# Attention rows carried as two fp16 halves from the softmax to the gate product

## The chip, the cores and the metric

The kernel runs on one core of a Trainium2 chip. Its engines are TensorE (PE, whose weight loads are listed as PEld), VectorE (DVE), ScalarE (ACT), GpSimd (POOL) and SyncE (SP, which here issues DMAs). The metric is the device time of one execution in microseconds (us); the time of a kernel is the median of its runs.

## What is computed

Three pieces follow one another: an attention with a window of 128 keys, a layer in which every token goes to one of eight experts, and a dense layer with a maximum of three products.

```python
# q, k, v: (4 batches, 8 heads, 576 tokens, 64)
scores = q @ k.T / 8 + slope[h] * -|i - j|, kept where 0 <= i - j < 128
x = softmax(scores) @ v                      # as (2304 tokens, 512)
logits = x @ w_gate + modality_bias[modality_id]
e = argmax(logits); gate = softmax(logits)[e]
y = gate * (relu(x @ w1[e]) @ w2[e])         # w1 512 x 1024, w2 1024 x 512
h = max(y @ g1, y @ g2, y @ g3)              # 512 x 768 each
out = h @ w_out                              # 768 x 512
```

All inputs are float32. The kernel gets close to float32 on TensorE's fp16 path by splitting an operand into two fp16 halves, high and low, and adding three products (high by high, high by low, low by high); the table PASSES names them.

## The kernel before

**Attention.** `Attention.run` (L485) walks over 36 groups: 4 batches, each with 4 tiles of 128 rows in two groups of four heads and one tile of 64 rows in one group. Round n does, in the order in which the code is written, the scores of a group (`qk`, L335), its softmax (L348 on DVE, L357 on ACT), the turning of the rows of the round before (`transpose`, L376, with `high` on ACT and `low` on DVE), the product with v of the group three rounds back (`pv`, L406 or, for 64 rows, L419), and `norm`, which divides by the row sums (L432 to L436) and leaves the attention rows in an SBUF tile `x` as float32. When both groups of a tile are done, SP stores `x` to a DRAM tile `xs` (L448; L443 for 64 rows). One round later (the same round for 64 rows) `xt` (L453) turns the tile on PE with four 128x128 transposes (L458), ACT copies it out of PSUM (L460), and in the round after that `logits` (L463) multiplies it with the float32 gate weights `wg` (L468), which takes eight float32 matmul instructions a tile.

**Fill.** Small chains of work (building the bias tables, routing the tokens) are Python generators. Each call of `fill()` lets every one of them put one step into the queues; softmax, `low` and the rest of `norm` call it at fixed points. So the number of `fill()` calls in a round sets how soon, in program order, the routing is done.

**Routing and gathering.** When the logits of a batch are there, `Route.select` sorts its tokens by expert. `begin` makes a `Batch` (units 0 to 3), whose `Gather.fetch` (L876) reads the token rows in expert order from `xs` with an indirect DMA issued by POOL (L880) into `xg`, 512 float32 a row. `place` (L886) turns them: in units 0 and 1 (`early`) by four PE transposes (L894), an ACT copy that rounds to the high half (L897) and a DVE subtraction for the low half (L898); in units 2 and 3 by an ACT copy (L902) and a DVE subtraction (L903) into `xc`, which `send` hands a turn later to a DMA transpose on SP (L910).

**Order of the whole.** Until batch 0 is routed and gathered only attention runs; from there on the experts' products of units 0 and 1 (`layer1`: L994, L1015) alternate with attention rounds, a piece of a round for each 1.1 units of product work (PACE). When the last round has been written, `settle` (L1367) ends the attention's memory pool and makes `Weights2`, which loads the dense layer's weights (L1070, L1076), puts their bits into float32 on DVE (L1110, L1115, L1121), and splits them on ACT and POOL (L1138 to L1140). `layer2(0)` (L1155, L1164, L1186, L1200) then needs them in their order; `w.tick()` writes the DVE steps between its products. Units 2 and 3, `layer2(1)` and a loop for rare leftovers come last. Every engine, and SP's queue of DMAs, takes its work strictly in the order written.

## Time and profile before

| | |
|---|---|
| time, median of 3 runs (lowest to highest) | 691.59 us (690.11 to 692.03) |
| the profiled execution's own time | 695.69 us |
| its span, first to last instruction | 693.9 us |
| mean granted TensorE clock | 0.979 of full |
| PE, DVE, ACT, POOL busy | 93%, 51%, 50%, 32% of the span |

The span falls into stages: attention alone up to 96 us; a short passage into the experts' products; attention and products mixed up to about 262 us; the end of `layer1(1)` up to 284 us; the first part of `layer2(0)` while its weights are still being prepared, up to 360 us; and from there products alone to 680 us. "Busy" of PE counts a matmul from its start to its modelled end, so matmuls overlap in it: how long one really costs is the distance from its start to the next one's. A bracket behind a row of the timeline tells how long the engine had been idle and what ended that.

### The profile page before, as it was taken

To read this page: it belongs to the slowest core of one execution; us is meant where nothing else is said; L and a number is where in the kernel's file an instruction comes from. 1 tells how busy PE (TensorE), PEld (TensorE's weight loads), DVE (VectorE), ACT (ScalarE), POOL (GpSimd) and SP (SyncE) were. 2 spreads that over 40 slices of the span, in tenths; PEclk is the share of its full clock that TensorE was granted. 3 is DMA by queue.
4 is the path that set the end of the run, shared out by engine and by line. 5 is a ranking of instruction groups with operands and counts; after the bars stand their busy time and mean duration, and the time that the engine had idled before them with its cause. 6 is when DMAs were issued, how large, how long until landed. Compare 5 with 4: busy or idle time off the path is not lost.

```text
span 693.9 us, 12894 instructions
## 1 busy us (share of the span) xinstructions
PE 644.1 (93%) x4787; PEld 401.9 (58%) x4787; DVE 351.8 (51%) x1083; ACT 346.3 (50%) x660; POOL 222.5 (32%) x232
## 2 busy tenths in 40 slices
PE   6899879999898989688899999999999999999993
PEld 4687756566665658354455564444447766656641
DVE  5977853875457656799971233062224455201100
ACT  5898876877777646645552211354647211111110
POOL 2111214524323213556662311482424111121121
PEclk9999988999999999899999999999999999999998
DMA  9655755345522237636833403344230000000011
GB/s 192 108 123 136 198 137 140 92 124 166 152 63 73 80 115 238 218 125 209 212 91 76 92 22 122 110 132 121 92 112 13 1 0 1 1 31 17 0 47 49
DMA packets 120800, 69.95 MB, mean 101 GB/s; under 512 B 68872, under 2 KB 115484, under 8 KB 120732
## 3 DMA queue, kind: packets, MB, share of 16 engines
q1 hardware_dynamic: 116992, 59.06, 32.0%
q0 software_dynamic: 3040, 9.96, 4.4%
q8 instruction: 40, 0.66, 0.4%
q14 instruction: 28, 0.23, 0.1%
q10 hardware_dynamic: 700, 0.04, 0.1%
HBM read 57.19 MB, written 9.44 MB: 96 GB/s over the span
## 4 chain that ended last, share of the span: by engine, by line
PE 71%; DVE 15%; ACT 7%; issue 3%; DMA 3%; POOL 0%; ACTq 0%; POOLq 0%; DVEq 0%
PE m L1155 22%; PE m L1015 12%; PE m L994 11%; PE m L1200 10%; PE s L335 4%; DVE b L1115 3%; PE m L376 3%; PE m L468 2%; PE bank L406 2%; PE m L283 2%; DMA st<-in_moe_w_dram 2%; DVE e L348 2%; DVE b L1121 1%; DVE b L1110 1%; ACT eh L382 1%
## 5 line engine op out<-in xcount | busy, mean ns | idle before, releaser
L1155 PEld LDWEIGHTS <-g 128*128 128x128 f16 x1296 | 128.1, 99 | 100.2 <-issue 12.7
L1155 PE MATMUL m<-yT,g 128*128 128x384 f16 x648 | 111.6, 336 | 11.9 <-ACT hx L1162 4.3
L1155 PE MATMUL m<-yh,g 128*128 128x384 f16 x648 | 105.7, 326 | 0.0
L966 DVE SCALAR_TENSOR_TENSOR wt<-st,wt 128x1024 f16<-128x1024 f32 x48 | 61.6, 1286 | 84.1 <-ACT wt L957 84.1
L1015 PE MATMUL m<-ht,wt 128*128 128x496 f16 (+3 forms) x576 | 101.9, 331 | 1.6 <-DVE wt L966 0.9
L1164 DVE SCALAR_TENSOR_TENSOR hx<-m,hx 128x384 f32<-128x384 f32 x72 | 39.8, 554 | 118.5 <-PE m L1155 117.9
L994 PEld LDWEIGHTS <-wt 128*128 128x128 f16 x576 | 54.6, 98 | 45.1 <-issue 3.2
L986 POOL TENSOR_TENSOR ht<-hf,ht 128x496 f16<-128x496 f32 (+3 forms) x48 | 50.1, 1049 | 86.7 <-ACT ht L985 78.5
L1015 PEld LDWEIGHTS <-wt 128*128 128x128 f16 x576 | 53.8, 98 | 39.3 <-DVE wt L966 1.1
L357 ACT ACTIVATE e<-e,nm 128x256 f32<-128x256 f32 (+2 forms) x144 | 59.8, 472 | 29.1 <-DVE nm L348 27.5
L984 ACT ACTIVATE hf<-m 128x496 f32<-128x496 f32 (+3 forms) x72 | 35.7, 496 | 59.0 <-PE m L1015 36.8
L994 PE MATMUL m<-xT,wt 128*128 128x496 f16 (+2 forms) x288 | 57.7, 341 | 3.1 <-ACT wt L957 1.6
L348 DVE CUSTOM_DVE_ANT_0 e<-s,bias 128x256 f32<-128x256 f32 (+1 forms) x128 | 46.0, 381 | 17.4 <-PE s L335 8.6
L957 ACT ACTIVATE wt<-st 128x1024 f16<-128x1024 f32 x48 | 50.0, 1045 | 4.3 <-DMA st<-in_moe_w_dram 4.2
L994 PE MATMUL m<-xh,wt 128*128 128x496 f16 (+1 forms) x288 | 51.1, 330 | 0.0
L387 DVE TENSOR_TENSOR el<-m,eh 128x512 f16<-128x512 f32 x64 | 42.4, 682 | 11.6 <-ACT eh L382 11.5
L335 PE MATMUL s<-kT,qT 64*128 64x256 f32 (+2 forms) x320 | 42.6, 384 | 3.3 <-DVE nm L348 2.2
L1186 POOL TENSOR_TENSOR xh<-hx,xh 128x384 f16<-128x384 f32 x18 | 16.4, 913 | 89.8 <-ACT xh L1185 89.8
L311 POOL TENSOR_TENSOR vl<-rawv,vh 128x512 f16<-128x512 f32 (+1 forms) x20 | 22.9, 1146 | 68.7 <-ACT vh L304 68.7
L1185 ACT ACTIVATE xh<-hx 128x384 f16<-128x384 f32 x18 | 9.4, 523 | 71.1 <-DVE hx L1164 67.1
L1206 ACT ACTIVATE ob<-m,gate 128x512 f32<-128x512 f32 x18 | 12.4, 687 | 55.0 <-PE m L1200 49.6
L382 ACT ACTIVATE eh<-m 128x512 f16<-128x512 f32 x64 | 34.8, 586 | 7.1 <-PE m L376 6.6
(184 smaller groups left out, 976.5 us busy)
## 6 DMA issues: line engine op xcount, KB each, us to landing
st<-in_moe_w_dram SPq DMA_DIRECT2D x66, 512.0 KB, 4.1
rawk<-in_k_dram SPq DMA_DIRECT2D x16, 256.0 KB, 3.3
rawq<-in_q_dram SPq DMA_DIRECT2D x16, 256.0 KB, 4.1
rawv<-in_v_dram SPq DMA_DIRECT2D x16, 256.0 KB
xs<-x SPq DMA_DIRECT2D x16, 256.0 KB, 2.1
st<-in_moe_w_out_dram SPq DMA_DIRECT2D x6, 512.0 KB, 6.3
rawk<-in_k_dram SPq DMA_DIRECT2D x4, 128.0 KB, 3.4
rawq<-in_q_dram SPq DMA_DIRECT2D x4, 128.0 KB, 4.9
```

What stands on the lines that cost most here:

```text
L335: nc.tensor.matmul(out=out[u][rows, x // 2, c0:c1], lhsT=self.qT[b, t][r, i, 0:n], rhs=self.kT[b][r, i, k0 + c0:k0 + c1], start=True, stop ...
L348: nc.vector.tensor_tensor_reduce(out=e[:, x, c0:c1], in0=s[x % 2][:, x // 2, c0:c1], in1=bias[:, x, c0:c1], scale=-0.125, scalar=3.0e38, o ...
L357: nc.scalar.activation(out=e[:, x, c0:c1], in_=e[:, x, c0:c1], func=ACTF.Exp, scale=-1.0, bias=nm[:, x:x + 1],)
L382: nc.scalar.activation(out=b, in_=a, func=ACTF.Copy)
L387: nc.vector.tensor_tensor(out=o, in0=a, in1=b, op=ALU.subtract)
L957: nc.scalar.activation(out=wt[:, 0], in_=st, func=ACTF.Copy, scale=SW)
L966: nc.vector.scalar_tensor_tensor(out=wt[:, 1], in0=st.rearrange("p (a b) -> p a b", a=a), scalar=SW, in1=wt[:, 0], op0=ALU.mult, op1=ALU.s ...
L986: nc.gpsimd.tensor_tensor(out=lo, in0=hf, in1=hi[1], op=ALU.subtract)
L994: nc.tensor.matmul(out=ps, lhsT=wt[:, wl, kk, o:o + 128], rhs=xT[:, xl, kk, bass.ds(d[0], cap)], start=(n == 0), stop=(n == 3 * KD - 1),)
L1015: nc.tensor.matmul(out=ps, lhsT=wt[:, wl, f, :], rhs=hs[f][:, xl], start=(n == 0), stop=(n == 3 * KF - 1),)
L1155: nc.tensor.matmul(out=ps, lhsT=w.g[:, wl, i, m, kk, :], rhs=yT[:, xl, kk, c:c + n2], start=(n == 0), stop=(n == 3 * KD - 1),)
L1200: nc.tensor.matmul(out=ps, lhsT=hm[:, xl, f, 128 * u:128 * u + 128], rhs=w.wo[:, wl, f, :], start=(n == 0), stop=(n == 3 * K2 - 1),)
```

## The change

From `norm` on, an attention row is kept as its two fp16 halves. `norm` writes the quotient to a scratch tile `xf`, DVE rounds it into the high half, POOL subtracts to get the low half; `x`, `xs` and `xg` hold 2 x 512 fp16 in place of 512 float32, which is the same number of bytes. `xt` turns eight fp16 blocks in place of four float32 ones, and ACT copies twice as many elements. The gate weights are split once, times 64, into `wgs`, and the logits are three fp16 products. `place` turns the halves as they are: early ones with eight PE transposes and two copies, late ones with a DMA transpose straight from `xg`; `xc`, its two instructions and `send` are gone. `norm` has one `yield`, and so one `fill()`, more.

```diff
@@ RouterConsts.bias
+            nc.vector.tensor_copy(ident16, ident)
+            yield
+            nc.vector.tensor_scalar(wgs[:, :, 0], wg, SW, None, ALU.mult)
+            yield
+            nc.vector.scalar_tensor_tensor(
+                out=wgs[:, :, 1], in0=wg, scalar=SW, in1=wgs[:, :, 0],
+                op0=ALU.mult, op1=ALU.subtract,
+            )
             yield 4
@@ norm
+            xf = p.tile([128, 4, D], F32, name="xf", tag="xf", bufs=2)
             nc.vector.tensor_tensor(
-                out=x[:, g], in0=ps[:, :, 0:D], in1=rd.to_broadcast([128, 4, D]),
-                op=ALU.mult,
-            )
+                out=xf, in0=ps[:, :, 0:D], in1=rd.to_broadcast([128, 4, D]), op=ALU.mult,
+            )
+            yield
+            nc.vector.tensor_copy(x[:, 0, g], xf)
+            nc.gpsimd.tensor_tensor(out=x[:, 1, g], in0=xf, in1=x[:, 0, g], op=ALU.subtract)
@@ xt
-            for kk in range(kd):
-                nc.tensor.transpose(ps[:, kk, :], xf[:, 128 * kk:128 * kk + 128], ident)
-            xt = self.p.tile([128, KD, 128], F32, name="xt", tag="xt", bufs=1)
-            nc.scalar.activation(out=xt[:, 0:kd], in_=ps[:, 0:kd], func=ACTF.Copy)
+            for l in range(2):
+                xf = x[:, l].rearrange("p a b c -> p (a b c)")
+                for kk in range(kd):
+                    nc.tensor.transpose(ps[:, l, kk, :], xf[:, 128 * kk:128 * kk + 128], ident16)
+            xt = self.p.tile([128, 2, KD, 128], F16, name="xt", tag="xt", bufs=1)
+            nc.scalar.activation(out=xt[:, :, 0:kd], in_=ps[:, :, 0:kd], func=ACTF.Copy)
@@ logits
-                nc.tensor.matmul(
-                    out=ps[0:m, 0:E], lhsT=xt[:, ku, m * u:m * u + m], rhs=wg[:, kk, :],
-                    start=(kk == 0), stop=(kk == KD - 1),
-                )
+                for i, (wl, xl) in enumerate(PASSES):
+                    nc.tensor.matmul(
+                        out=ps[0:m, 0:E], lhsT=xt[:, xl, ku, m * u:m * u + m],
+                        rhs=wgs[:, kk, wl, :],
+                        start=(kk == i == 0), stop=(kk == KD - 1 and i == 2),
+                    )
@@ Gather.place
-                xc = self.tile([128, 2, DM], F16, "xc")
-                nc.scalar.activation(out=xc[:, 0], in_=xg, func=ACTF.Copy)
-                nc.vector.tensor_tensor(out=xc[:, 1], in0=xg, in1=xc[:, 0], op=ALU.subtract)
-                self.out.append((xc, t))
...
+                    self.eng[self.sent % len(self.eng)].dma_start_transpose(
+                        out=o.rearrange("p a k n -> p (a k) n"), in_=xg[0:o.shape[3]],
+                    )
```

The scheduling code then puts work in another order. Three places matter here; line numbers of the changed kernel lie 8 to 22 above those of before.

On DVE, at the end of each attention round (here early in attention alone), `norm` has one instruction more. Before:

```order
L434 RECIPROCAL rd<-rd 128x4
L436 TENSOR_TENSOR x<-bank,rd 128x256
L387 TENSOR_TENSOR el<-m,eh 128x512
L479 SCALAR_TENSOR_TENSOR L_85<-m,mbt 64x8
L479 SCALAR_TENSOR_TENSOR L_85<-m,mbt 128x8
```

Now:

```order
L445 RECIPROCAL rd<-rd 128x4
L448 TENSOR_TENSOR xf<-bank,rd 128x256
L452 CAST x<-xf 128x256
L398 TENSOR_TENSOR el<-m,eh 128x512
L498 SCALAR_TENSOR_TENSOR L_87<-m,mbt 64x8
L498 SCALAR_TENSOR_TENSOR L_87<-m,mbt 128x8
```

The rounding to fp16 stands between the division and the subtraction for the next group's low half.

On ACT, where attention alone ends: `e` are softmax rows (one row for a group), `xT` the gathered token rows, `wt` expert weights, `hf` and `ht` results of the experts' products. Before:

```order
L303 ACTIVATE rawv<-rawv 128x512
L304 ACTIVATE vh<-rawv 128x8x64
L297 ACTIVATE kT<-m 128x4x128
L357 ACTIVATE e<-e,nm 128x128 x4
L382 ACTIVATE eh<-m 128x512
L297 ACTIVATE qT<-m 128x512
L897 ACTIVATE xT_753<-m 128x4x128 x3
L897 ACTIVATE xT_753<-m 128x4x112
L957 ACTIVATE wt<-st 128x1024 x3
L357 ACTIVATE e<-e,nm 128x256 x4
```

Now:

```order
L314 ACTIVATE rawv<-rawv 128x512
L315 ACTIVATE vh<-rawv 128x8x64
L308 ACTIVATE kT<-m 128x4x128
L918 ACTIVATE xT_789<-m 128x4x128 x3
L918 ACTIVATE xT_789<-m 128x4x112
L965 ACTIVATE wt<-st 128x1024 x3
L368 ACTIVATE e<-e,nm 128x128 x4
L992 ACTIVATE hf<-m 128x496
L993 ACTIVATE ht<-hf 128x496
L393 ACTIVATE eh<-m 128x512
```

The token rows of batch 0 are placed one group earlier, behind the 19th group in place of the 20th. The rest of attention shifts with it: before, its last turned tile stands behind 24 results of the experts' products, now behind 28 of the 36.

On SP, where attention ends: the first four loads of `Weights2` are the rows L1070 (L1078 now), the loads of expert weights L948 (L956 now). Before:

```order
L443 DMA xs_74<-x 64x256 x2
L948 ISA
L948 DMA st<-in_moe_w_dram 128x8x128
L948 ISA
L948 DMA st<-in_moe_w_dram 128x8x128
L948 ISA
L948 DMA st<-in_moe_w_dram 128x8x128
L1070 DMA st_4361<-in_moe_w_dram 128x4x256
L1070 DMA st_4363<-in_moe_w_dram 128x4x256
```

Now:

```order
L457 DMA xs_74<-x 128x1x256 x2
L956 ISA
L956 DMA st<-in_moe_w_dram 128x8x128
L956 ISA
L956 DMA st<-in_moe_w_dram 128x8x128
L1037 TENSOR_LOAD slot_e_101
L1037 ISA x2
L956 ISA
L956 DMA st<-in_moe_w_dram 128x4x256
L1078 DMA st_4829<-in_moe_w_dram 128x4x256
L1078 DMA st_4831<-in_moe_w_dram 128x4x256
```

The loads for the dense layer come two expert loads later: behind the last load for unit 1 and the first for unit 2.

## Rows read from the trace of the kernel before

**Rows 1.** The page, busy time, share of the span and instructions of each engine.

```profile
PE 644.1 (93%) x4787; PEld 401.9 (58%) x4787; DVE 351.8 (51%) x1083; ACT 346.3 (50%) x660; POOL 222.5 (32%) x232
```

**Rows 2.** Busy by stage: PE, PEld, DVE, ACT, POOL; then clock, DMA share, GB/s.

```profile
20.00:96.00 76.00, 68.10 (x833) 56.75 (x833) 58.80 (x271) 64.67 (x145) 15.83 (x23) 0.98 0.61 146
...
104.00:262.00 158.00, 150.86 (x1427) 99.61 (x1427) 95.67 (x350) 110.45 (x210) 51.69 (x51) 0.99 0.39 111
...
284.00:360.00 76.00, 62.97 (x360) 35.90 (x361) 71.05 (x122) 37.46 (x70) 48.86 (x38) 0.91 0.59 176
360.00:680.00 320.00, 319.96 (x1846) 177.48 (x1845) 92.85 (x241) 100.54 (x174) 91.05 (x90) 1.00 0.19 55
```

**Rows 3.** The chain of waits from 20 to 96 us, shares by engine and line.

```profile
by line: PE m L376 9.7%; PE s L335 9.7%; ACT e L357 7.8%; ACT eh L382 7.5%; PE bank L406 7.5%; DVE e L348 7.2%; PE m L468 6.6%; PE m L283 6.0%; DVE el L387 5.7%; PE m L458 4.1%; DVE biast L152 3.4%; ACT vh L304 3.3%; ACT rawv L303 2.9%; DVE
```

**Rows 4.** Timeline of ACT: exponentials of two groups, 16 groups apart (start, duration).

```profile
21.26 1.69 ACT L357 ACTIVATE e<-e,nm 128x256 f32<-128x256 f32 x4
...
93.95 1.26 ACT L357 ACTIVATE e<-e,nm 128x128 f32<-128x128 f32 x4
```

**Rows 5.** Busy time by stretch of L468, the logits, alone: PE, PEld.

```profile
0.00:96.00 96.00, 7.97 (x64) 7.32 (x64) 0.98 0.73 155
96.00:284.00 188.00, 11.39 (x97) 10.41 (x96) 0.98 0.43 125
```

**Rows 6.** Timeline of PE around 275 us: short 16-bit matmuls back to back.

```profile
275.54 0.40 PE L657 MATMUL bank<-r_ge,ones 128*128 128x8 bf16 x10
275.79 0.20 PE L660 MATMUL bank<-r_oh,tri 128*128 128x80 bf16 x1
...
276.07 0.52 PE L666 MATMUL bank<-r_gt,ones 128*128 128x80 bf16 x10
276.42 2.46 PE L1015 MATMUL m<-ht,wt 128*128 128x224 f16 x24
```

**Rows 7.** The chain of waits, mixed stage: what a group's PE work takes back to back.

```profile
228.05 1.06 PE s L335 x8
229.11 0.83 PE bank L406 x24
...
231.16 0.87 PE m L376 x8
```

**Rows 8.** Groups of instructions by form: busy, mean ns of one, idle before.

```profile
L957 ACT ACTIVATE wt<-st 128x1024 f16<-128x1024 f32 x48 | 50.0, 1045 | 4.3 <-DMA st<-in_moe_w_dram 4.2
...
L311 POOL TENSOR_TENSOR vl<-rawv,vh 128x512 f16<-128x512 f32 x16 | 18.4, 1151 | 49.8 <-ACT vh L304 49.8
...
L460 ACT ACTIVATE xt<-m 128x512 f32<-128x512 f32 x16 | 9.5, 591 | 2.5 <-PE m L458 2.5
...
L903 DVE TENSOR_TENSOR xc<-xg,xc 128x512 f16<-128x512 f32 x10 | 9.2, 956 | 10.8 <-ACT xc L902 10.8
...
L152 DVE TENSOR_SCALAR bias<-c_rel 128x256 bf16<-128x256 f32 x8 | 2.0, 287 | 0.0
```

**Rows 9.** Who waited for whom: us in total, times, longest.

```profile
POOL ht L986 <- ACT ht L985: 78.5, 32, 14.8
```

**Rows 10.** Timeline around 284 us, SP's queue and PE.

```profile
266.83 2.54 SPq L1070 DMA_DIRECT2D st<-in_moe_w_dram  x4
...
279.62 0.36 PE L1015 MATMUL m<-ht,wt 128*128 128x224 f16 x2 [0.73 <-ACT wt L957]
...
285.31 0.82 PE L1155 MATMUL m<-yT,g 128*128 128x384 f16 x2 [2.15 <-ACT g L1139]
289.06 16.91 PE L1155 MATMUL m<-yT,g 128*128 128x384 f16 x94 [2.93 <-POOL g L1140]
```

**Rows 11.** Timeline, DVE and PE, while the dense weights are prepared.

```profile
326.87 2.73 DVE L903 TENSOR_TENSOR xc<-xg,xc 128x512 f16<-128x512 f32 x2 [1.10 <-ACT xc L902]
...
333.28 11.93 PE L1155 MATMUL m<-yT,g 128*128 128x384 f16 x63 [2.88 <-ACT hx L1162]
...
359.81 13.81 PE L1155 MATMUL m<-yT,g 128*128 128x384 f16 x84 [1.44 <-ACT hx L1162]
```

More of the change, by code (lines that the diff above doesn't have):

```diff
@@ L44 @@
 PLACES = 2
+PASSES = ((0, 0), (0, 1), (1, 0))
 @with_exitstack
@@ L75, in windowed_attention_moe_kernel @@
     bank = psV.tile([128, 512], F32, name="bank")
-    xs = [dram.tile([HALF, DM], F32, name=f"xs{h}") for h in range(2)]
+    xs = [dram.tile([HALF, 2 * DM], F16, name=f"xs{h}") for h in range(2)]
     ident = const.tile([128, 128], F32, name="ident")
@@ L85, in windowed_attention_moe_kernel @@
     ones_r = const.tile([1, 128], F16, name="ones_r")
+    ident16 = const.tile([128, 128], F16, name="ident16")
     wg = const.tile([128, KD, E], F32, name="wg")
+    wgs = const.tile([128, KD, 2, E], F16, name="wgs")
     mbt = const.tile([128, B, NTB, E], F32, name="mbt")
@@ L428, in norm @@
             if g == 0:
-                self.xs[b, t] = p.tile([128, 2, 4, D], F32, name="x", tag="x", bufs=2)
+                self.xs[b, t] = p.tile([128, 2, 2, 4, D], F16, name="x", tag="x", bufs=2)
             x = self.xs[b, t]
@@ L443, in norm @@
                     nc.sync.dma_start(
-                        out=dst[r + 512:r + S, 256 * u:256 * u + 256],
-                        in_=x[64 * u:64 * u + 64, 0].rearrange("p b c -> p (b c)"),
+                        out=dst[r + 512:r + S, :].rearrange("r (l c) -> r l c", l=2)[
+                            :, :, 256 * u:256 * u + 256
+                        ],
+                        in_=x[64 * u:64 * u + 64, :, 0].rearrange("p l b c -> p l (b c)"),
                     )
@@ L449, in norm @@
                     out=dst[r + 128 * t:r + 128 * t + 128, :],
-                    in_=x.rearrange("p a b c -> p (a b c)"),
+                    in_=x.rearrange("p l a b c -> p (l a b c)"),
                 )
@@ L479, in logit_out @@
             nc.vector.scalar_tensor_tensor(
-                out=L[b // 2][0:m, NTB * (b % 2) + t, :], in0=ps[0:m, 0:E], scalar=1.0 / SX,
+                out=L[b // 2][0:m, NTB * (b % 2) + t, :], in0=ps[0:m, 0:E], scalar=1.0 / (SX * SW),
                 in1=mbt[0:m, b, t, :], op0=ALU.mult, op1=ALU.add,
@@ L867, in __init__ @@
             self.pool, self.xT, self.own = pool, xT, own
-            self.q, self.out = [], []
+            self.q = []
             self.eng, self.sent = eng, 0
@@ L876, in fetch @@
         def fetch(self, src, idx, t, early=False, **kw):
-            xg = self.tile([128, DM], F32, "xg")
+            xg = self.tile([128, 2 * DM], F16, "xg")
             if kw:
```

33 lines of the change are left out of this document (10 added, 23 removed).

## The prediction

> **What bounds the kernel now.** I read the page's busy line first, then busy time by stage, then the chain of waits inside a stage. PE is busy 93% of the span [rows 1], but not everywhere for the same reason [rows 2]. From 360 to 680 us it has no gap (319.96 of 320 us); the attention rows are no longer touched there except by work that lies beside it, so nothing of this change counts after 360 us. From 284 to 360 us PE is busy 63.0 of 76 us and DVE 71.1: DVE, preparing the dense weights, is the bound. From 104 to 262 us PE is, with 150.9 of 158 us, while DVE has 62 us and ACT 48 us to spare. In attention alone, 20 to 96 us, no engine is the bound by itself: PE 68.1, ACT 64.7, DVE 58.8 of 76 us, and the chain goes from one to the next, with the logits L468 at 6.6% of it [rows 3]. So the change is costed by stage.
>
> **The change, part by part.** The sum is made against the profiled execution (695.69 us, of which 693.9 are the span). That one lies 4.1 us above the median of the runs shown, 691.59; I take the same saving off the median.
>
> *Logits on PE.* They cost 8.0 us before 96 us and 11.4 us after it [rows 5]: 161 records, eight a tile, about 0.12 us each. Now a tile takes twelve fp16 matmuls with 8 columns. The nearest rows for those: ten bf16 matmuls with 8 columns start at 275.54 and the next line at 275.79, 0.025 us each [rows 6]; 24 fp16 ones with new weights each time and 64 or 65 columns take 0.83 us at most, 0.035 us [rows 7]. I take 0.028 us, as the columns are those of the first row and the changing weights those of the second: 12 x 0.028 = 0.33 us a tile. For the 8 tiles before 96 us this is 2.6 us in place of 8.0, for the 12 after it 4.0 in place of 11.4.
> Where an instruction of TensorE has so few columns, the Trainium skill (TensorE: Matmul & The Clock Gate, section "Wait — 56ns, not 53.3ns?") gives a floor of about 25 ns from start to start, and of about 62 ns per matmul when the instructions are decoded in software; the trace agrees with the first (0.025 us). By the second, a tile would cost 0.74 us by estimate and the gain of the logits would fall by more than half.
>
> *Turning.* Four float32 transposes of 128 columns become eight fp16 ones, for 20 tiles in `xt` and 10 early tiles in `place`. Float32: 0.87 us for eight, 0.109 us each [rows 7], 0.44 us a tile. Fp16 with 128 columns is not in the trace; it lies between 80 columns at 0.035 us (276.07 to 276.42, ten) and 224 columns at about 0.10 us (24 in 2.46) [rows 6]. On the line between them 128 columns are 0.057 us, 0.46 us a tile: nothing gained or lost. The ends would give 0.28 and 0.80 us a tile, over 30 tiles -5 to +11 us, of which I keep ±3 for the range, since both ends have other widths.
>
> *In attention alone* (before 96 us). PE loses 5.4 us; of the chain it holds 6.6% of 76 us = 5.0 us [rows 3], so about two thirds of that, 3.4 us, can come off the end. Against it stand two additions. DVE rounds to fp16 once a group: 128x256 float32 to 16 bits took 0.287 us [rows 8], and 16 groups get there, 4.6 us. ACT copies 1024 elements a tile in place of 512: 1.045 in place of 0.591 us [rows 8], for 7 full tiles 3.2 us, and about 0.3 for the half one. These 8 us lie on engines that are 77% and 85% busy [rows 2]; I count under half as late, 3.4 us, so the stage's pace stays as it is. Bounds: all of the gain and none of the cost, -3.4; all of the cost and no gain, +8. POOL's subtraction is half of the 512-element one, 1.151 us [rows 8], so about 0.6 us; POOL is busy 15.8 of 76 us, and turning comes a round later, so it hides. The three instructions for `ident16` and `wgs` replace nothing but fit into idle DVE time.
>
> *One group moved.* The extra `fill()` brings the routing of batch 0 one group sooner, so 19 groups run alone in place of 20. A group alone takes (93.95 - 21.26) / 16 = 4.54 us [rows 4]. In the mixed stage it costs PE its own work: scores 1.06, turning 0.87, products with v 0.83 [rows 7], half a tile's logits and `xt` (0.17 and 0.23), and the turning of q and k at the same 0.109 us, 0.44: 3.6 us. Gain 0.9, say 1.0 us with the slack that PE keeps. Bounds 0 and 4.5.
>
> *In the mixed stage.* PE-bound, so the logits' 7.4 us come off the end in full. DVE and ACT carry the roundings (20 x 0.29) and the longer copies in their idle 62 and 48 us. New is a wait: PE's turning of a low half waits for POOL, and `xf` has two buffers, so DVE's division waits for the subtraction two groups back; behind PE then stand the experts' products, behind DVE the next softmax. For tiles of 128 rows a round (about 9 us) lies between; for the three 64-row tiles nothing does, and each can cost POOL's own 0.6 us. I take 1.5 us, bounds 0 and 20 (below). Net -5.9 us.
>
> *The seam at 262 to 290 us.* The first loads of the dense weights come two expert loads later on SP, and attention ends four products later, some 5.5 us of PE work (12 matmuls a product at 0.10 to 0.12 us). Before, they left at 266.83 us and held up the expert weights, so PE waited 0.73 us for a weight, then 2.15 and 2.93 us for the first dense ones [rows 10]. Now the expert weights go first and the dense ones start closer to their use. The two cancel to within what I can read: 0, bounds -4 (these waits gone) and +6 (the 5.5 us uncovered).
>
> *Late gathers.* `xc` goes: ten ACT copies and ten DVE subtractions of 0.956 us [rows 8]. Four of the ten lie before 360 us. The first two, 2.73 us after a wait of 1.10 for ACT, stand in DVE's bound stretch, and PE's gap behind them is 2.88 us; behind the other two it is 1.44 [rows 11]. More than PE's gaps cannot be won: -4.3 us. Bounds 0 and -7 (with the clock, 0.91 in this stage [rows 2], at full). The other six cover nothing that ends late. The DMA transposes stay, a turn earlier; SP's loads of w_out now stand behind two of them, and are needed only after the first products.
>
> Sum: 0 - 1.0 - 5.9 + 0 - 4.3 = -11.2 us; 695.7 becomes 684.5, the median 691.6 becomes 680.4, **680 us**.
>
> **The rivals.** *The seam opens*: the dense weights arrive 5.5 us late and DVE's bound stretch begins that much later; 680 + 6 = 686. For it: the order on SP; against it: DVE has fewer steps waiting in front. *Attention alone gets slower by all that is added* (+8 in place of 0) and the rest of the gain holds: 680 + 8 = 688; with a bit of the seam, 690, no change. For it speaks ACT at 85%. *POOL comes before PE* (the other side): in the mixed stage POOL already waits 2.45 us a time for ACT (78.5 us, 32 times) [rows 9] and takes its work in order, so a low half can stand behind an expert's low half. If each of the 12 tiles there waits for one such instruction of about 1.1 us and its own 0.6 us, PE loses 12 x 1.7 = 20 us, the time is 680 - 1.5 + 20 = 699. It decides from about 1.0 us of PE waiting a tile. Against it: the round between, in which the queue empties (POOL is busy 51.7 of 158 us).
> The Trainium skill (SBUF — State Buffer, section "Who interferes with whom") adds that a DVE copy in a two-port mode and GpSimd lock each other out; no row here shows a rounding beside a subtraction, and it would feed the second rival. *The change doesn't do what it says*: if the early order of routing brought no group forward, 1 us is lost, inside the range.
>
> **How the numbers follow.** Forecast (680) 0.60; seam 0.15; slower attention 0.13; POOL before PE 0.12. The range, 671 to 691, takes the first three: at the low end the bounds of attention alone (-3), turning (-3) and clock (-3), at the high end the second rival with a part of the seam. A measurement here tells 0.3%, 2 us, from no change, so faster means below 689.5: the forecast and the seam, and a small part of the third, 0.76; within, 0.12; slower 0.12.
>
> **What would show it.** Right: L468's successor near 0.33 us a tile; the first expert product some 4 us sooner; PE's gaps at 330 and 358 us gone. Wrong: PE idle before turning `x` with POOL as releaser; exponentials of 16 groups further apart than 72.7 us; PE's gap before the first dense product over 6 us.

## The result, and the profile after

The changed kernel takes 695.92 us (692.97 to 696.18) where the kernel before takes 691.36 (690.11 to 692.03), a ratio of 1.0057 with an interval from 1.0035 to 1.0078. It is **0.6% slower**; 1.7% faster had been forecast, and the time lies above the range.

The two profiled executions tell it the other way round: 695.69 us before, 692.97 after. The first is 4 us above the median of its kernel, the second 3 us below. Executions of one kernel differ, among other things, in how long TensorE's granted clock stood at half (1.2 of 2.4 GHz): up to the end of PE's work 13.7 us in the profile of after, but 34.2 us in that of a second execution of the same kernel (a_again, below), in stretches at changing places. That is not the whole difference: the profiles of before and of b_again, which are one kernel, both have 23.9 us at half clock, and took 695.69 and 693.43 us. So below, sizes are taken from medians, from ratios or from stretches at full clock, and places and causes from traces.

The page of after, PE, PEld, DVE, ACT and POOL, beside [rows 1]:

```profile
PE 632.6 (92%) x4979; PEld 390.8 (57%) x4979; DVE 358.0 (52%) x1112; ACT 350.1 (51%) x650; POOL 256.0 (37%) x268
```

By stage, beside [rows 2], the columns as there:

```profile
20.00:96.00 76.00, 63.45 (x855) 50.66 (x856) 61.54 (x271) 65.75 (x139) 24.83 (x38) 0.98 0.58 140
104.00:262.00 158.00, 147.23 (x1500) 94.36 (x1499) 106.49 (x382) 116.83 (x216) 74.20 (x72) 0.99 0.40 108
284.00:360.00 76.00, 63.54 (x406) 37.26 (x407) 73.44 (x123) 38.37 (x71) 51.06 (x38) 0.96 0.62 186
```

PE has less to do (632.6 us in place of 644.1) and, in the first two stages, is idle for longer: 12.6 us in place of 7.9 from 20 to 96 us, 10.8 in place of 7.1 from 104 to 262. In these two stages together PE waits 8.3 us more, against 11.5 us of work that were taken off it.

The chain of waits from 20 to 96 us, shares by engine and line, beside [rows 3]:

```profile
by line: DVE el L398 11.3%; PE m L387 8.8%; DVE e L359 8.1%; PE bank L417 7.7%; PE m L294 6.5%; issue 5.9%; PE s L346 5.4%; ACT xt L477 5.1%; DVE xf L448 4.9%; DVE x L452 4.6%; ACT vh L315 3.3%; ACT rawv L314 3.2%; PE m L475 2.8%; ACT eh L3
```

The logits, 6.6% of it before, are no longer among the lines printed. In their place stand the division into `xf` (4.9%), the rounding (4.6%) and the copy `xt` (5.1%); `el`, the low half that DVE makes behind division and rounding, has gone from 5.7 to 11.3%. In the lines printed PE's share falls from 43.6 to 31.2% and DVE's rises from 16.3 to 28.9%: a part of the chain has moved from PE to DVE.

At the end of attention (timeline of after, beside [rows 10]; PE's last products, SP's loads of the dense weights, ACT's expert weight and what is behind it, PE's first dense product):

```profile
273.50 9.36 PE L1023 MATMUL m<-ht,wt 128*128 128x224 f16 x96
274.39 2.03 SPq L1078 DMA_DIRECT2D st<-in_moe_w_dram  x4
276.77 7.37 SPq L956 DMA_DIRECT2D st<-in_moe_w_dram  x3
...
286.10 1.06 ACT L965 ACTIVATE wt<-st 128x1024 f16<-128x1024 f32 x1 [4.67 <-DMA st<-in_moe_w_dram]
...
287.76 0.63 ACT L1146 ACTIVATE b<-b 128x512 f32<-128x512 f32 x1
288.42 0.63 ACT L1147 ACTIVATE g<-b 128x512 f16<-128x512 f32 x1
...
289.11 0.82 PE L1163 MATMUL m<-yT,g 128*128 128x384 f16 x2 [6.25 <-ACT g L1147]
```

The four loads leave at 274.39 us, before at 266.83. ACT then stands 4.67 us for an expert weight of unit 2 that was issued behind them (at 276.77, landed at 286.02), and the split of the first dense weight stands behind that in ACT's queue. PE, done at 282.86, waits 6.25 us. In the kernel before ACT waits 4.22 us for the same reason, but 7.6 us earlier, while PE still has products (timeline of before, ACT):

```profile
278.50 1.06 ACT L957 ACTIVATE wt<-st 128x1024 f16<-128x1024 f32 x1 [4.22 <-DMA st<-in_moe_w_dram]
```

### The profile page after: what moved, and what is told of

The parts are those of the page before. It is cut to its first block, busy times and chain, and to the rows that moved or that the text cites. A ratio compares the mean times of both kernels' runs of the same rounds, so it can differ in the third digit from the quotient of the medians.

```text
span 691.2 us, 13333 instructions
## 1 busy us (share of the span) xinstructions
PE 632.6 (92%) x4979; PEld 390.8 (57%) x4979; DVE 358.0 (52%) x1112; ACT 350.1 (51%) x650; POOL 256.0 (37%) x268
## 4 chain that ended last, share of the span: by engine, by line
PE 70%; DVE 17%; ACT 6%; DMA 3%; issue 2%; POOL 0%; SPq 0%; DVEq 0%; POOLq 0%; ACTq 0%
PE m L1163 22%; PE m L1002 13%; PE m L1023 12%; PE m L1208 10%; PE s L346 3%; DVE b L1123 3%; PE bank L417 2%; DMA st<-in_moe_w_dram 2%; PE m L387 2%; PE m L294 2%; DVE b L1129 2%; DVE e L359 2%; DVE el L398 2%; DVE b L1118 1%; ACT xt L477 1%
## 5 line engine op out<-in xcount | busy, mean ns | idle before, releaser
L1163 PEld LDWEIGHTS <-g 128*128 128x128 f16 x1296 | 127.0, 98 | 98.5 <-issue 8.0
L1163 PE MATMUL m<-yT,g 128*128 128x384 f16 x648 | 108.9, 329 | 12.2 <-ACT g L1147 6.2
L453 POOL TENSOR_TENSOR x<-xf,x 128x256 f16<-128x256 f32 x36 | 31.2, 865 | 118.2 <-DVE x L452 83.8
L387 PE MATMUL m<-ident,e 128*128 128x128 f32 (+1 forms) x256 | 36.4, 282 | 2.8 <-DVE el L398 1.7
```

What stands on the lines that cost most here:

```text
L387: nc.tensor.transpose(ps[:n, x, :], e[:, x, a:z], ident)
L1163: nc.tensor.matmul(out=ps, lhsT=w.g[:, wl, i, m, kk, :], rhs=yT[:, xl, kk, c:c + n2], start=(n == 0), stop=(n == 3 * KD - 1),)
```

## Experiments

In the labels `b_` is the kernel before with one thing added, `a_` the changed kernel with one thing altered, `n_` the changed kernel without its additional `yield`, with more altered (n_bestyield has the `yield` back). The suffix 2 and `again` mean the same kernel once more. All were set against runs of the kernel before on the same chip; the ratio is to these. A price in us is a difference of ratios times the time of the kernel before, unless medians are named. For the places, five points were read from each trace. "Nine groups" is the distance between the exponentials of the 64-row groups of batches 0 and 1, a stretch without half clock unless a * stands at it; "products" runs from the first expert product to the beginning of PE's wait ahead of the first dense one.

| kernel | ratio (95% interval) | nine groups | first expert product | products | first dense product | first with w_out |
|---|---|---|---|---|---|---|
| b_again | 0.9984 (0.9967 to 1.0002) | 37.75 | 98.45 | 184.4 | 284.98 | 371.31 |
| a_again | 1.0047 (1.0032 to 1.0061) | 39.72 | 106.15 | 182.6 | 295.48 | 377.43 |
| a_noyield | 0.9949 (0.9927 to 0.9970) | 39.26 | 104.33 | 178.9 | 285.36 | 370.01 |
| a_poolcast | 0.9995 (0.9977 to 1.0013) | 40.40 * | 105.69 | 182.5 | 294.56 | 377.11 |
| b_yield | 1.0073 (1.0057 to 1.0089) | 38.20 | 93.95 | 188.3 | 288.25 | 374.69 |
| b_halves | 1.0067 (1.0042 to 1.0092) | 38.92 | 102.42 | 180.6 | 285.13 | 373.26 |
| b_cast | 1.0053 (1.0032 to 1.0073) | 40.84 | 105.63 | 181.0 | 288.79 | 376.95 |
| b_sub | 0.9999 (0.9982 to 1.0017) | 38.04 | 101.46 | 181.4 | 285.00 | 373.25 |
| b_logits2 | 1.0288 (1.0255 to 1.0320) | 43.45 * | 107.65 | 195.4 | 305.18 | 393.49 |
| n_const | 0.9937 (0.9917 to 0.9957) | 39.27 | 102.35 | 177.3 | 281.82 | 366.48 |
| n_copy32 | 0.9913 (0.9894 to 0.9932) | 38.16 | 100.80 | 177.6 | 280.51 | 365.07 |
| n_poolcast | 0.9956 (0.9936 to 0.9976) | 40.44 * | 104.06 | 179.3 | 285.53 | 370.18 |
| n_best | 0.9897 (0.9880 to 0.9915) | 38.17 | 99.44 | 176.9 | 278.52 | 363.17 |
| n_best2 | 0.9899 (0.9884 to 0.9913) | 38.18 | 99.61 | 176.8 | 278.60 | 363.26 |
| n_bestyield | 0.9910 (0.9885 to 0.9936) | 38.93 | 102.93 | 181.7 | 291.77 | 372.78 |
| n_bestyield2 | 0.9984 (0.9969 to 0.9998) | 38.95 | 98.89 | 181.3 | 286.77 | 368.57 |
| n_bestact | 0.9934 (0.9912 to 0.9955) | 40.25 * | 101.27 | 178.2 | 281.64 | 366.36 |
| n_bestdve | 1.0055 (1.0032 to 1.0078) | 43.65 | 111.69 | 176.3 | 290.14 | 374.78 |

In the kernels with the additional yield (a_again, a_poolcast, b_yield, n_bestyield, n_bestyield2) 19 groups run before the first expert product, in the others 20. From the first product with `w_out` on all are alike, 320 us to the end.

The places are of one execution each, and the first expert product scatters most: two executions of one kernel have it at 101.19 and 98.45 us (before, b_again), at 100.72 and 106.15 (after, a_again) and at 102.93 and 98.89 (n_bestyield, n_bestyield2). By itself a difference of a few microseconds there shows little. And b_again is the kernel before itself: its 0.9984 shows how far a ratio can lie off by chance.

### Both kernels once more

> The changed kernel, unchanged. Its profiled execution took 692.97 us at a granted clock of 0.984, its other runs 695.9 to 696.2 at 0.977 to 0.979. Theory 'the clock': runs differ by stretches of half clock, so the new runs lie between 692.5 and 696.5 us and their spans rise with falling clock, about 3 us for 0.007. Rival 'real scatter': spans differ at equal clock by over 1 us.

> The kernel before, unchanged. Its profiled execution took 695.69 us at 0.979, the timed ones 690.1 to 692.0. Theory 'the clock': runs near 691 us show a clock of 0.985 or more, and the profile then shows fewer of the stretches at half clock that the first profile has near 91, 101 to 108, 285 to 292, 309 and 333 us. Rival: the same stretches, and the 4 us lie elsewhere.

On this chip the kernel before took 695.39 us, the changed one 699.04, and all runs of a_again lie above the range that had been expected. Both theories were half right: b_again's runs go from 692.8 us at a clock of 0.979 to 695.9 at 0.974, and a_again's slowest run shows the lowest clock, but at one clock, 0.976, runs of the kernel before still differ by 3.2 us. The clock is part of the scatter, not all of it. The chip is another part: at a clock of 0.979 the kernel before took 692.8 to 695.4 us here and 690.1 to 691.9 us on the chip of n_best2. The profile of a_again shows what an execution can have that the profile of after has not (busy time by stretch, columns as above):

```profile
28.00:32.00 4.00, 4.00 (x36) 3.36 (x36) 3.74 (x17) 3.31 (x8) 0.00 (x1) 0.50 0.78 193
32.00:36.00 4.00, 3.94 (x23) 2.99 (x20) 2.47 (x9) 1.83 (x3) 1.79 (x3) 0.50 0.32 71
...
88.00:92.00 4.00, 1.70 (x25) 1.24 (x24) 1.32 (x6) 2.57 (x6) 3.39 (x5) 0.92 1.12 336
92.00:96.00 4.00, 2.82 (x28) 2.76 (x29) 2.51 (x10) 2.01 (x5) 2.15 (x4) 0.50 0.88 290
```

From 26.5 to 40.1 us PE is granted half its clock and is busy for 12.6 of the 13.6 us. Ahead of that it had waited 1.46 us for DVE. At 88 to 92 us, while 336 GB/s are loaded, PE, DVE and ACT all stand for a time; ACT's last exponential there waits 0.89 us for nothing that the profile shows. The execution of after has no such stop: from 88 to 92 us it loads 344 GB/s, and PE is busy for 3.70 of the 4 us. So the rate of the loads alone does not make the stop.

### The additional yield

```diff
                 out=xf, in0=ps[:, :, 0:D], in1=rd.to_broadcast([128, 4, D]), op=ALU.mult,
             )
-            yield
             nc.vector.tensor_copy(x[:, 0, g], xf)
```

> The changed kernel without the additional yield in norm: the rounding follows the division at once, and there is no additional fill() in a round; so batch 0 is placed after 20 groups again, as before. Theory 'fill on DVE': the additional step of routing work stands on DVE in front of the rounding and of the next low half el, for which PE waits; without it attention alone goes back towards 4.12 us a group (from 4.36), -3 to -4 us, while the group that had moved costs +1 back: 692 to 693 us against 696. Rival 'the added instructions': the rounding on DVE and the longer ACT copy make the pace, and the time rises by the group moved back, 696 to 698 us.

The time went from 699.04 to 691.70 us, the ratio from 1.0047 to 0.9949: one `yield` holds 6.8 us (7.3 by the medians), and without it the change is a gain. Half of my reason was right: nine groups fell only from 39.72 to 39.26 us, so most of the price is elsewhere. PE's gap ahead of the first dense product is 2.15 us again.

```diff
                 op=ALU.mult,
             )
+            yield
             dst, r = xs[b // 2], S * (b % 2)
```

(b_yield: the same in the kernel before, alone.)

> The kernel before with nothing but the additional yield at the end of norm, so one fill() more in a round: 19 groups alone and the dense loads two expert loads later, as in the changed kernel. Theory 'the yield costs at the seam what it gives ahead of it': batch 0 is gathered a group earlier (first expert product 3 to 4 us sooner), the mixed stage is longer by that group (3.6 us), and at the seam ACT stands at an expert weight that lands late, with the dense weights behind it: PE waits 6 us in place of 2.2; +2 to +5 us in all, ratio 1.003 to 1.007. Rival 'the yield harms only with the rounding behind it': ratio 0.998 to 1.002.

1.0073: 5.1 us, with nothing else changed. The first expert product comes 4.5 us sooner than in b_again, where 3 to 4 had been foretold; the products take 3.9 us longer than in b_again and 7.7 longer than in b_halves (which has no half clock there, while b_yield has it up to 101.6 us and again at 197); the dense part begins 6.0 us behind the last product in place of 2.2.

### The pair: rounding and subtraction

```diff
+            xh = p.tile([128, 2, 4, D], F16, name="xh", tag="xh", bufs=2)
+            nc.vector.tensor_copy(xh[:, 0], x[:, g])
+            nc.gpsimd.tensor_tensor(out=xh[:, 1], in0=x[:, g], in1=xh[:, 0], op=ALU.subtract)
```

(b_halves; b_cast is without the third line, b_sub without the second and with `x - x` in the third.)

> The kernel before, with the changed kernel's pair of instructions added in each group: after the division DVE rounds x to fp16 and POOL subtracts, into a scratch tile that nobody reads. All else is as before, float32 logits included. This prices the pair alone. Theory 'attention alone pays for what is added': the nine groups of batch 1 (37.7 us in the kernel before, 39.2 without the additional yield, 39.7 in the changed kernel) take 39 us or more, and the time rises by 4 to 6 us. Rival 'the pair hides, the wide ACT copy and the start-up constants cost': under 38.2 us, time +0 to +2 us.

> The kernel before with only the rounding to fp16 on DVE added in each group, into a scratch tile that nobody reads; no subtraction on POOL. Rounding and subtraction together cost 0.67% and brought the first expert product from 98.4 to 102.4 us. Theory 'DVE time': 16 roundings of 0.29 us in front of el come off in full, first product 3 to 4 us later, ratio 1.004 to 1.006. Rival 'the two engines' meetings': it is POOL's subtraction that holds DVE up (0.29 becomes 0.8 to 1.1 us in some), and the rounding alone costs 1.000 to 1.003.

> The kernel before with only POOL's subtraction added in each group (x minus x, into a scratch tile), no rounding on DVE. Theory 'DVE time': POOL has 60 us to spare in attention alone, ratio 0.999 to 1.001. Rival 'meetings': 1.003 to 1.006, with single DVE instructions of more than 1 us beside it.

The pair costs 0.67%, 4.7 us. POOL's subtraction costs nothing (0.9999), the rounding alone 0.53%. So what counts is the rounding, which stands in DVE's queue ahead of `el`. What b_cast adds is a finding by itself: its nine groups are longer than those with the pair (40.84 and 38.92 us). The timeline of b_cast, DVE and POOL, shows why:

```profile
42.54 1.12 POOL L311 TENSOR_TENSOR vl<-rawv,vh 64x512 f16<-64x512 f32 x1 [12.82 <-ACT vh L304]
42.89 0.92 DVE L441 CAST xh<-x 128x256 f16<-128x256 f32 x1
...
47.23 1.13 POOL L311 TENSOR_TENSOR vl<-rawv,vh 128x512 f16<-128x512 f32 x1 [3.35 <-ACT vh L304]
47.50 1.08 DVE L441 CAST xh<-x 128x256 f16<-128x256 f32 x1
...
55.65 0.42 DVE L436 TENSOR_TENSOR x<-bank,rd 128x256 f32<-128x256 f32 x1
55.69 1.12 POOL L311 TENSOR_TENSOR vl<-rawv,vh 128x512 f16<-128x512 f32 x1 [7.26 <-ACT vh L304]
56.11 0.92 DVE L441 CAST xh<-x 128x256 f16<-128x256 f32 x1
```

A rounding that takes 0.29 us by itself, begun while POOL makes the low half of v, ends 0.15 to 0.22 us behind POOL's instruction. With the pair the two seldom meet: POOL's subtraction waits for the rounding, and the low half of v stands behind the subtraction (in b_halves a rounding at 45.64 us, the subtraction at 46.01, the low half of v at 46.69). Of the 17 roundings ahead of 100 us six take over 0.5 us in b_cast, one in b_halves.

### Where else could the rounding go

```diff
-            nc.vector.tensor_copy(x[:, 0, g], xf)
+            nc.gpsimd.tensor_copy(x[:, 0, g], xf)
```

(a_poolcast with the yield, n_poolcast without it.)

> The changed kernel with the rounding on POOL in place of DVE; POOL then makes both halves, one after the other. Theory 'DVE and its meetings with POOL': DVE is freed of 36 roundings (12.4 us busy, up to 1.14 us one by one where POOL works) that stand in front of el, and of the hand-over to POOL: attention alone 3 us shorter, mixed stage 1 to 2 us, time 691 to 693. Rival 'POOL late': POOL needs about 1.1 us or more for both halves and stands behind the experts' low halves, PE waits for it before turning x: 696 to 700.

> The changed kernel without the additional yield, and with the rounding on POOL as well. With the yield, moving the rounding to POOL gave 3.5 us (699.0 to 695.5). Theory 'the rounding is a load on DVE': it gives 2 to 3.5 us here too (ratio to before 0.990 to 0.992). Rival 'it only undid the harm of the yield' (where the rounding stood behind a step of routing): under 1 us, 0.994 to 0.996.

With the yield it gave 0.5%, 3.6 us, somewhat less than the theory's 4 to 5; without the yield it gave nothing (0.9956 against 0.9949), and nine groups took 1.2 us more (a stretch of half clock in them). That is what the rival foretold: it had only taken the rounding out from behind the routing's step. On ACT (n_bestact, below) it cost 0.4%.

### Constants and the wide copy

```diff
-            nc.vector.tensor_copy(ident16, ident)
-            yield
-            nc.vector.tensor_scalar(wgs[:, :, 0], wg, SW, None, ALU.mult)
-            yield
-            nc.vector.scalar_tensor_tensor(
...
+            nc.gpsimd.tensor_copy(ident16, ident)
+            nc.gpsimd.tensor_scalar(wg, wg, SW, None, ALU.mult)
+            nc.gpsimd.tensor_copy(wgs[:, :, 0], wg)
+            nc.gpsimd.tensor_tensor(out=wgs[:, :, 1], in0=wg, in1=wgs[:, :, 0], op=ALU.subtract)
```

> The changed kernel without the additional yield, and with the constants ident16 and wgs made on POOL, without steps of their own, in place of three DVE instructions with two yields. From 20 to 32 us DVE is 96% busy with tables; theory 'start-up': the constants and the roundings there push PE into a wait of 1.5 us and its clock to half from 26 us on (6.8 to 13.7 us long); without the constants the stretch from the exponentials of group 3 to those of group 8 goes from 26.4 us back towards 24, time -1 to -3 us against a_noyield (ratio to before 0.991 to 0.993 where that had 0.9949). Rival 'the roundings do it alone': no change, 0.995.

0.9937 against 0.9949: 0.8 us, with intervals that overlap, so it is not settled by the time. From the exponentials of group 3 to those of group 8 the trace shows no gain (26.5 us against 26.3); group 3 itself begins a microsecond sooner.

```diff
-            nc.scalar.activation(out=xt[:, :, 0:kd], in_=ps[:, :, 0:kd], func=ACTF.Copy)
+            nc.scalar.activation(
+                out=xt.bitcast(F32)[:, :, 0:kd], in_=ps.bitcast(F32)[:, :, 0:kd], func=ACTF.Copy
+            )
```

> The changed kernel without the additional yield, and with the copy of the turned halves out of PSUM read as pairs: 512 float32 words in place of 1024 fp16 numbers. This prices the wide copy: it should fall from 1.02 to about 0.6 us, as the copy of 512 float32 took before. Theory 'the wide copy is on the chain': PE's waits for xt shrink by 0.4 us a tile; batch 1's nine groups from 39.2 to about 38 us, and the time falls by 3 to 6 us (ratio to before near 0.988). Rival 'it lies beside other work': under 1 us.

0.9913, 2.5 us less than without it; somewhat under what was expected, on the side of the theory. Groups of instructions by form, of after and of n_copy32:

```profile
L477 ACT ACTIVATE xt<-m 128x1024 f16<-128x1024 f16 x16 | 16.3, 1018 | 3.7 <-PE m L475 3.6
```

```profile
L476 ACT ACTIVATE xt<-m 128x512 f32<-128x512 f32 x16 | 9.5, 592 | 3.0 <-PE m L474 3.0
```

The same bytes as half as many words: 1018 ns become 592, and nine groups 39.26 become 38.16.

### What PE's time is worth

```diff
-            for kk in range(KD):
+            for kk in 2 * list(range(KD)):
```

> The kernel before with every logits product made twice: 16 float32 matmuls a tile in place of 8, the second pass starts the sum anew. It prices PE time by stage: 8 tiles of about 0.92 us (0.56 for 64 rows) before the first expert product, some 6.5 us, and 12 tiles in the mixed stage, some 9.9 us. Theory 'PE's time comes off in full where PE is the bound, and by half to two thirds in attention alone': mixed stage +9 to +10 us, first product +3 to +4.5 us, time +13 us (ratio 1.019). Rival 'the mixed stage has slack too': mixed +5 to +6 us, ratio near 1.012.

2.9%, 20 us, more than either theory gave, for 7.0 us of matmuls ahead of the first expert product and 10.0 behind it (0.92 us a full tile, 0.56 one of 64 rows). The first product comes 9.2 us later than in b_again, the products take 11 us longer than in b_again and 15 longer than in b_halves. The trace also has more stretches at half clock (one from 63 to 70 us, within the nine groups). In neither stage does PE's time hide.

### Together

n_best is n_const with the copy of n_copy32.

> The changed kernel without the additional yield, with the constants made on POOL and the narrow copy of the turned halves. Of the three, the yield's removal gave 1.0% (1.0047 to 0.9949), the copy 0.36% more and the constants 0.12% more. If these add up: ratio 0.990, about 688 where before is 695.4. Rival 'both took the same wait out': 0.991 to 0.992, like the copy alone.

```diff
-            nc.vector.tensor_copy(x[:, 0, g], xf)
+            nc.scalar.activation(out=x[:, 0, g], in_=xf, func=ACTF.Copy)
```

> As n_best, with the rounding to fp16 on ACT in place of DVE, one ACT instruction more in a group. The pair of rounding and subtraction alone cost 0.67% in the kernel before, while on POOL the rounding took more (nine groups of batch 1: 40.4 us against 39.3). Theory 'DVE is now what attention alone waits for' (its lines lead the chain of n_copy32 from 40 to 85 us): nine groups from 38.2 to under 37.5 us, ratio 0.986 to 0.988. Rival 'ACT is as full as DVE': 38.2 us or more, ratio 0.990 or above.

```diff
-            nc.gpsimd.tensor_tensor(out=x[:, 1, g], in0=xf, in1=x[:, 0, g], op=ALU.subtract)
+            nc.vector.tensor_tensor(out=x[:, 1, g], in0=xf, in1=x[:, 0, g], op=ALU.subtract)
```

> As n_best, with the subtraction for the low half on DVE, behind the rounding, in place of POOL. Theory 'DVE time': 36 subtractions of 256 elements, some 0.4 us each on DVE, add 16 times 0.4 = 6 us in attention alone; ratio 0.996 to 0.999 where n_best has 0.990. Rival 'meetings': without POOL's part DVE's rounding never waits, ratio 0.990 or below.

n_best, without the yield, with both edits above, has 0.9897 (0.9880 to 0.9915), and once more 0.9899: **1.0% faster than the kernel before**, 684.97 us beside 691.59. The gains added up. The rounding on ACT loses 0.4% of that, the subtraction on DVE 1.6%, more than either theory had: nine groups take 43.65 us there, 5.5 more, for nine subtractions of 0.42 us and for roundings that meet POOL (three of them take 0.82 to 1.15 us). So what is added on DVE is paid for in full and more; but the rounding gained nothing on POOL and lost on ACT, so DVE is not the one bound of attention alone.

```diff
+            yield
             nc.vector.tensor_copy(x[:, 0, g], xf)
```

> As n_best, with the additional yield of the changed kernel back. In the kernel before the yield alone cost 0.73%, in the changed kernel its removal gave 1.0%. Theory 'the yield's price stands by itself, at the seam': 0.7 to 1.0% here too, ratio 0.997 to 1.000, with PE's gap ahead of the first dense product at 6 us in place of 2.2. Rival 'with the copy and the constants out of the way the earlier group pays': ratio 0.988 to 0.992.

Its median was 688.87 us beside 695.35, a ratio of 0.9910 (0.9885 to 0.9936), with single runs up to 694.85 us. The time is the rival's; PE's gap ahead of the first dense product, 7.14 us, is the theory's. Beside the 0.9897 of n_best, which ran on another chip, the yield would cost 0.1% here. No n_best had run beside it, so the two were set side by side, unaltered:

> n_best once more, beside its twin with the yield on one chip. Expected 0.988 to 0.991 of before.

> n_bestyield once more, beside n_best on one chip. In its first look most runs were at 688 to 689 us where n_best would be at 688.8 by its ratio, but the profiled one was at 694.85 with a clock of 0.977. Theory 'the yield costs only where PE's clock falls': runs at a clock of 0.985 equal n_best within 1 us, runs at 0.98 or below are 3 to 6 us longer, and their profile shows stretches at half clock near 91 and 105 us that n_best has not. Rival 'a price of its own': all its runs lie 3 us or more above those of n_best.

Here the yield costs 0.85%, by the medians 5.4 us, and every run of n_bestyield2 lies 2.4 us or more above the slowest of n_best2, also at the same clock. That is nearly the rival's condition (3 us): the yield has a price of its own on this chip. How large it is on the chip of n_bestyield was not measured. Timeline of PE, n_best2 and n_bestyield2: the first products with experts' weights, dense weights, and w_out.

```profile
99.61 0.59 PE L999 MATMUL m<-xT,wt 128*128 128x496 f16 x2 [1.58 <-ACT wt L962]
...
278.60 0.50 PE L1160 MATMUL m<-yT,g 128*128 128x384 f16 x2 [2.15 <-ACT g L1144]
...
363.26 11.82 PE L1205 MATMUL m<-wo,yh 128*128 128x512 f16 x54
```

```profile
98.89 0.59 PE L1000 MATMUL m<-xT,wt 128*128 128x496 f16 x2 [1.58 <-ACT wt L963]
...
286.77 0.82 PE L1161 MATMUL m<-yT,g 128*128 128x384 f16 x2 [6.61 <-ACT g L1145]
...
368.57 11.82 PE L1206 MATMUL m<-wo,yh 128*128 128x512 f16 x54
```

One group fewer runs ahead of the first product, but that comes 0.7 us sooner, not 4.5; the products take 4.5 us longer, not 3.6; and from their end to w_out it is 88.4 us in place of 86.8. So the yield adds 4.5 - 0.7 = 3.8 us ahead of the first product, 4.5 - 3.6 = 0.9 in the mixed stage and 1.6 behind it, 6.3 in all; less the 4.5 - 3.6 that the moved group does give, 5.4. This splits one pair of executions, and n_bestyield2 stood at half clock for 3.4 us more than n_best2 ahead of the first product and for about as much more in the mixed stage, so only the last of the three parts is free of the clock.

## Why the prediction was wrong, step by step

By the ratios the changed kernel lies 3.3 us (0.47%) above the kernel before on the second chip. What was added has its prices from experiments: the yield 6.8 us, the pair 4.7, the wide copy 2.5, the constants perhaps 0.8, together 14.8. No run has the gains from logits and late gathers by themselves; what is left for them is 14.8 - 3.3 = 11.5 us. They had been put at 15.1 (3.4 + 7.4 + 4.3), what was added at 3.4 + 1.5, and the moved group at -1.0. Without the yield, at a ratio of 0.9949, the time would by estimate have been 688 us, inside the range.

**One group moved, -1.0 us: wrong sign, the step that decided.** The `fill()` was taken as a change of order with one group's worth in it. The order was read rightly (19 groups for 20, attention's end four products later, the dense loads two expert loads later), its size was not: +6.8 us in this kernel, +5.1 in the kernel before. What was left out is that a step more a round delays work at each point that it shifts. Ahead of the first product attention gets longer at equal groups (3.8 us in n_bestyield2, a part of it half clock). A step that stands on DVE ahead of the rounding and of `el` is seen in five of the 19 rounds there (in after at 26.6 us and from 67.6 to 82.8), with 0.15 to 0.35 us each, which is less than half of that; what the rest waits for is not shown. In the mixed stage 0.9 us remain, which the clock may hold. And the seam opens (1.2 to 2.1 us in the kernels with the yield and fp16 rows).

**The seam, 0: somewhat too low; the rival had the gap right, and its price too high.** It had been priced at +6 with a chance of 0.15, and its sign named, a gap over 6 us. The gap is 6.25 us. But what is late are not the dense weights on DVE: it is an expert weight behind them on SP's queue, which ACT meets first. And two thirds of the added 4.1 us come back: from the end of the products to w_out it is 88.0 us in after, 86.8 in a_noyield, which has the gap of 2.15. That DVE prepares on while PE waits, so that PE's later waits shrink, fits with this and was not measured by itself.

**In attention alone, 0: mis-sized.** Without the yield, nine groups at full clock take 39.26 us in place of 37.75 (b_again). (Up to the first product it is 104.3 us in a_noyield in place of 98.5 and 101.2 in b_again and before, but a_noyield has 10.2 us of half clock ahead of it, these two 0.1 and 3.7.) The instructions were sized rightly: roundings of 0.29 us, copies of 1.02. The weight was wrong: "under half" of 8 us was charged because DVE and ACT are 77% and 85% busy over the stage. The runs show 4.7 us for the pair and 2.5 for the copy over the whole kernel, of which 1.3 lie in the mixed stage (below), so some 6 of the 8. A stage whose chain goes from engine to engine has no cover for an instruction that stands in that chain, and the rounding stands between the division and `el`. Against it the logits give 0.8 us in nine groups (38.92 in b_halves, 38.16 in n_copy32, which has the pair and the narrow copy), about half of what had been counted. So the cost came nearer to its bound than to the half that was taken, while the gain was about half.

That the three constants "fit into idle DVE time" had no row behind it. From 20 to 32 us DVE is busy 11.63 of 12 us (b_again). What they cost stays unsettled.

**Logits and turning: right by the piece, partly wrong in the sum.** Timeline of PE, after:

```profile
254.87 0.61 PE L475 MATMUL m<-ident,x 128*128 128x128 f16 x8
255.32 1.38 PE L1023 MATMUL m<-ht,wt 128*128 128x480 f16 x6
256.60 0.46 PE L486 MATMUL m<-wgs,xt 128*128 128x8 f16 x12
256.91 0.19 PE L417 MATMUL bank<-vh,eh 128*128 128x65 f16 x1
```

Twelve logits matmuls take 0.31 us (0.33 foretold), eight transposes 0.45 (0.46 foretold). By the 62 ns that the Trainium skill gives for instructions decoded in software (TensorE: Matmul & The Clock Gate, section "Wait — 56ns, not 53.3ns?") the twelve would by estimate have been 0.74; the trace agrees with its floor of 25 ns (0.31 us for twelve, 26 ns each). What they replace was overstated: 11.4 us is busy time [rows 5], in which neighbours overlap and which counts tiles of 64 rows like full ones. From start to start a full tile took 0.92 us and one of 64 rows 0.56; now they take 0.31 and 0.48, so that 9 full and 3 half tiles save 9 x 0.61 + 3 x 0.08 = 5.7 us, not 7.4.

**In the mixed stage, -5.9 us: right sign, a bit over half.** The clean pair is b_halves (180.6 us) and n_const (177.3), both at full clock there: -3.3 us. Busy time by stretch, columns as above, of b_halves and of n_const:

```profile
102.00:279.00 177.00, 167.63 (x1611) 114.43 (x1611) 119.14 (x400) 122.43 (x234) 79.77 (x78) 1.00 0.44 125
```

```profile
102.00:279.00 177.00, 165.07 (x1744) 110.71 (x1745) 120.97 (x402) 130.06 (x240) 80.72 (x80) 1.00 0.46 127
```

PE's waits for `xt` from 102 to 280 us (us in total, times, longest), of b_halves, of n_const and of n_copy32:

```profile
PE m L471 <- ACT xt L463: 3.5, 3, 1.9
```

```profile
PE m L481 <- ACT xt L472: 4.8, 3, 2.3
```

```profile
PE m L487 <- ACT xt L476: 3.5, 3, 1.9
```

ACT's longer copy comes back as 1.3 us of PE waiting, which go again with the narrow one (in time this does not show: 177.6 us in n_copy32, which has 3.4 us of half clock there, 177.3 in n_const): the copies were said to lie in idle time, and that holds for ACT's load but not for the tiles whose logits follow at once. With these 1.3 of the 5.7 us, 4.4 were to be had; where the last microsecond went is open.

**POOL before PE** (the rival on the slow side, 0.12): did not happen. No wait of PE in the mixed stage of after names POOL's subtraction, although that took 1.00 us in the mean there and up to 1.83. The 1.5 us taken for such waits were not needed either, and the rounding adds nothing there (180.6 us with it in b_halves, 181.4 without in b_sub).

**Late gathers, -4.3 us: right, somewhat smaller.** From the end of the products to w_out it is 88.5 to 90.4 us in the kernels with `xc` (b_again, b_sub, b_halves) and 86.7 to 86.9 in those without it that have no additional yield. That is -1.7 to -3.6 us; the other three with `xc` and without the yield (before, b_cast, b_logits2) lie at 90.3 to 90.5 us, so the upper end is the likelier. PE's gaps there, beside [rows 11], timeline of after:

```profile
331.44 8.16 PE L1163 MATMUL m<-yT,g 128*128 128x384 f16 x48 [0.66 <-ACT hx L1170]
...
345.31 25.74 PE L1163 MATMUL m<-yT,g 128*128 128x384 f16 x156 [1.38 <-ACT hx L1170]
```

The gap of 2.88 us has shrunk to 0.66; the other stayed. From 284 to 360 us DVE is busy for 73.4 of 76 us now, so it is still the bound.

**The range and the signs.** Of the three signs named for "wrong" two came: the exponentials further apart (69.8 us over 15 groups in after, 65.9 in before; the sixteenth now lies behind the first expert product) and the gap over 6 us. The first product came 0.5 us sooner in the profiles shown where 4 had been said. The two cases, a slower attention and the open seam, were held to be alternatives with 0.13 and 0.15. The seam comes from the added `fill()`, the slower attention from that and from the added instructions; nothing kept the two apart, and they came together.

**What stays open.** How much of the yield's price is half clock and how much is waiting was not separated, and its size differs from one pair to the next. Nor was it tried what the engines wait for at 88 to 92 us in a_again. An order that keeps the earlier group and loads the dense weights in time was not tried.

## What to carry to other kernels

A step added to a generator is a change of schedule at every point where something counts its steps; cost it first, on every queue that it shifts, and try the edit without it, since here one `yield` turned a gain of 0.5% into a loss of 0.5%. Where a stage has no single bound, charge an added instruction nearly in full if it stands in front of something that the chain of waits names, however idle its engine is on the average. And before trusting two profiles against each other, compare their own times with the medians of their kernels.

## What the runs showed of the hardware

In the three rows of b_cast a DVE rounding from SBUF to SBUF does not run beside a two-operand instruction of POOL: 0.29 us became 0.92 to 1.08 and ended just behind POOL's. In turn POOL's subtraction, 0.67 us by itself, takes 1.42 to 1.83 us eight times in after, each time beside DVE's low half of an expert weight (timeline of after, DVE and POOL):

```profile
125.09 1.21 DVE L974 SCALAR_TENSOR_TENSOR wt<-st,wt 128x1024 f16<-128x1024 f32 x1
...
125.40 1.42 POOL L453 TENSOR_TENSOR x<-xf,x 128x256 f16<-128x256 f32 x1 [0.38 <-DVE x L452]
```

The division on DVE, which reads PSUM, kept its 0.42 us beside the same work of POOL (the row at 55.65 us). The Trainium skill (SBUF — State Buffer, section "Who interferes with whom") says that the engine that issues first gets the shared ports and the other blocks for that whole instruction; the trace agrees for the rounding. The prediction had counted this toward its second rival only, in which the rounding indeed stood.

The time of ACT's copy out of PSUM goes by the number of elements, not by bytes: 1024 fp16 took 1018 ns, the same 2 KB a partition as 512 float32 words 592 ns, and 512 fp16 (the 64-row tile) 597 ns.

The same wait of PE, 1.46 us for DVE at 25 us, was followed by half clock in a_again (13.7 us of it) and a_noyield (6.8 us), and by full clock for the next scores in n_copy32. The wait alone does not say whether an execution gets such a stretch.
